# Moving the transposes of x behind the closing scores in a band and stride attention before an MoE, with padded tiles and split loads

## The chip, the cores and the metric

The kernel runs on one core of a Trainium2 chip. A core has five engines with their own instruction queues: TensorE (matmuls and transposes), VectorE, ScalarE, GpSimd and SyncE, which here only issues DMAs. The metric is device time in microseconds. The program was run three times for its median; one further execution was profiled, and all rows of the profile come from that one.

## The reference

Attention with eight batches, eight heads, 576 positions and 64 features; four heads see a local band of 32 positions, four see every 32nd position. The result goes, as 4608 tokens of 512 features, through a router with eight experts of limited capacity (tokens taken in the order of their logits over all tokens) and through two matrices for each expert.

```python
pos = np.arange(S)
rel = pos[:, None] - pos[None, :]
mask_local = (rel >= 0) & (rel < stride)
mask_strided = (rel >= 0) & (pos[None, :] % stride == pos[:, None] % stride)
masks = np.stack([mask_local if h < H // 2 else mask_strided for h in range(H)], axis=0)
scores = scale * np.matmul(q, k.transpose(0, 1, 3, 2))
scores = np.where(masks[None, :, :, :], scores, -1000000000.0)
attn = np.exp(scores - np.max(scores, axis=-1, keepdims=True))
attn = attn / (np.sum(attn, axis=-1, keepdims=True) + 1e-09)
x = np.matmul(attn, v).transpose(0, 2, 1, 3).reshape(B * S, H * D)
...
logits = x @ w_gate
order = np.argsort(-logits.flatten())
...
for e in range(E):
    mask = assigned == e
    out[mask] = np.maximum(x[mask] @ w1[e], 0.0) @ w2[e]
```

## The kernel before

The first third of the time is the attention, the rest routing and experts; the change is in the attention alone, and the engines' order in the rest is the same before and after.

**Units and steps.** Each batch is two units, a strided one (`xs`, `v_s`, `ks`, `qs` in names) and a local one (`xl`, `v_l`, `kl`, `ql`). A unit has two head pairs, and a pair is one step: 32 steps, in the order strided pair 0, strided pair 1, local pair 0, local pair 1, batch after batch. The loop is at lines 612 to 678, and its order is written by hand: no scheduler moves an instruction, each engine runs its queue in that order, and waits only for what an instruction needs. A strided head is cut into tiles of 54 queries (`SQ`), the last of a half being 18 (`SLAST`, from `wide`); a local head into tiles of 32 queries and 64 keys.

**What a step does.** On TensorE, step i: `close_scores` of pair i+1 (`dots`, the scores' last tiles into a two-bank tile `spa`; VectorE then takes the maxima with a transpose, L333), `mix` of pair i for the first head (probabilities `pr` by values, into `po`), `turn` of pair i-1 (x is transposed into `xt`, for the router's logits), `max_t` of pair i+1 (the maxima `mx` are transposed, L339; then VectorE: L342, the cast to bf16 at L344, its error at L345, and `dd` at L347), `mix` for the second head, `open_scores` of pair i+2 (the mask as a matmul, L318, and the first tiles of scores), sometimes a sum of squares `total_v` (L271) or `logits` (L519), and `shift` of pair i+1 (L352: minus the maximum, as a matmul from `dd`). ScalarE then takes the exponential of pair i+1 (L356).

**ScalarE's queue** is, after an exponential: a square of the values (L268, in three steps of four), the copies of the gates (L467 and L455, to `lt`), the finish copy of x to fp16 (L403), and then in the next step the copy of the turn (L438, `keep`). GpSimd subtracts the fp16 copy from x (L404) behind the finish copy, for the low part.

**The banks of the accumulation memory (PSUM).** `ps_a` has two tiles of two banks (`spa`), `po` takes two banks, and `ps_b` has two tiles of one bank (`spb`). The turn uses the tile `a`, which step i opens for the scores of pair i+2; the mask that opens these scores can only be written when ScalarE has copied the turn out of it. The gates (L464), `total_v`, `logits` and the turn of the first pair (`turn_first`) use `spb`. A tile `warm_o` is taken from `ps_b` ahead of the loop (L608) and is written by matmuls without a reader ahead of the first step, between the first ones, and once more in step 31.

**Loads.** SyncE's queue issues the transfers: queries, keys and values of a unit ahead of their use (values to fixed buffers `vbuf`, L299), and ahead of the loop seven tables for the routing (`late_constants`, 0.86 MB with 0.59 MB for `iota`).

Of the kernel before, what the change touches and what calls it, by code (L numbers as in the profile page):

```python
# [8 lines left out]
F32 = mybir.dt.float32  # L9
# [3 lines left out]
AF = mybir.ActivationFunctionType  # L13
# [16 lines left out]
BANK = 512  # L30
OPEN_S, OPEN_L = 1, 3
MAX_FIRST = True
WARM = {(-2, 0): 11, (-1, 0): 3, (-1, 2): 3, (31, 0): 2}
# [99 lines left out]
def band_stride_attention_then_capacity_moe(ctx, tc, qt, kl, ks, nl, ns, wg, w1, w2, cst, out, dbg=None):  # L133
# [83 lines left out]
    with tc.tile_pool(name="ld", bufs=2) as ld, \  # L217
# [13 lines left out]
        po_all = ps_o.tile([128, 2, BANK], F32, name="po")  # L231
        nc.vector.memset(po_all, 0.0)
        for g in "sl":
# [11 lines left out]
        class Unit:  # L245
# [39 lines left out]
            def load(u, parts=(slice(0, 2),), v=True):  # L285
                b, g = u.b, u.g
                if v:
                    u.load_v()
                u.kt = ld.tile([128, 2, u.nk], F32, name="k" + g)
                u.q = ld.tile([128, 2, S], F32, name="q" + g)  # L290
                for p in parts:
                    nc.sync.dma_start(u.kt[:, p], (ks if u.strided else kl)[b, :, p])
                    nc.sync.dma_start(u.q[:, p], qt[b, :, u.p0 + p.start:u.p0 + p.stop])

            def load_v(u):
                u.vn = vbuf[u.g, u.b % 2]
                for f in range(2):
                    r = slice(64 * f, 64 * f + SQ) if u.strided else slice(64 * f + 32, 64 * f + 64)
                    nc.sync.dma_start(u.vn[r], (ns if u.strided else nl)[u.b, f])  # L299

# [20 lines left out]
            def dots(u, p, ts_):  # L321
                for t in ts_:
                    n = u.wide(t)
                    o = u.nq * t
                    for f, h in ((0, 0), (1, 1), (0, 1), (1, 0)):
                        c = HS * f + SQ * t if u.strided else LQ * (2 * t + f)
                        m = n if u.strided else LK
                        r = slice(64 * h, 64 * h + 64)
                        nc.tensor.matmul(u.sp[p][64 * f:64 * f + m, h, o:o + n], u.kt[r, p, c:c + m], u.q[r, p, c:c + n],
                                         start=False, stop=False, skip_group_check=True)  # L330
# [5 lines left out]
            def max_t(u, p):  # L336
                pm = u.sp[p][:, 1, HS:HS + 64]
                for k in range(4):
                    nc.tensor.matmul(pm[32 * k:32 * k + 32], mxb[u.g, p], ident[:, 64 * (k % 2):64 * (k % 2) + 64],  # L339
                                     start=False, stop=False, skip_group_check=True)  # L340
                mr = wk.tile([128, 32], F32, name="mr")
                nc.vector.tensor_reduce(mr, pm.rearrange("r (g c) -> r c g", c=32), axis=AX.X, op=OP.max)  # L342
                mh = wk.tile([128, 32], BF16, name="mh")
                nc.vector.tensor_copy(mh, mr)  # L344
                nc.vector.tensor_tensor(mh[64:], mr[64:], mh[64:], op=OP.subtract)  # L345
                u.dd = wk.tile([128, NB, 32], BF16, name="dd")
                nc.vector.tensor_tensor(u.dd, mh[:, None, :].to_broadcast([128, NB, 32]), bm, op=OP.mult)  # L347

            def shift(u, p):
                df = u.dd.rearrange("r n c -> r (n c)")  # L350
                for h in range(2):
                    nc.tensor.matmul(u.sp[p][:, h, :HS], sel, df[:, HS * h:HS * h + HS], start=False, stop=True,  # L352
                                     skip_group_check=True)
                pr = wk.tile([128, S], F32, name="pr")
                u.pr[p] = pr
                nc.scalar.activation(pr.rearrange("k (h n) -> k h n", h=2), u.sp[p][:, :, :HS], AF.Exp, scale=0.125)  # L356

# [4 lines left out]
            def mix(u, p, h, ts_=None, po=None):  # L362
# [5 lines left out]
                for t in range(u.nt) if ts_ is None else ts_:  # L368
                    n, o = u.wide(t), u.place(t, h)
                    for f in range(2):  # L370
                        j, r = (t, 64 * f) if u.strided else (t // 2, 64 * (t % 2) + 32 * f)
                        k = slice(64 * f, 64 * f + 64)
                        nc.tensor.matmul(po[r:r + n, j - j0], pr[k, o:o + n], u.vn[k, t, 2 * p + h],  # L373
                                         start=(j == j0), stop=(j == j1 - 1), skip_group_check=True)
# [47 lines left out]

            def turn(u, p, po):
                if u.b not in xtb:
                    xtb[u.b] = wk.tile([128, H // 2, S], F32, name="xt")
                for j, c, t, r in u.pieces():
                    x = u.x[r, t, 2 * p:2 * p + 2].rearrange("q h d -> q (h d)")
                    nc.tensor.transpose(po[:, j, c:c + r.stop - r.start], x, ident[r, r])

            def pieces(u):  # L430
                if u.strided:
                    return [(f, SQ * t, t, slice(64 * f, 64 * f + u.wide(t))) for t in range(u.nt) for f in range(2)]
                return [(0, EV + 128 * j, j, slice(0, 128)) for j in range(3)] + \
                    [(1, 128 * (j - 2), j, slice(0, min(128, S - 128 * j))) for j in range(2, u.nx)]

            def keep(u, p, po):
                o = 0 if u.strided else EV
                nc.scalar.activation(xtb[u.b][:, 2 * u.strided + p].rearrange("d (j n) -> d j n", j=2), po[:, :, o:o + HB],  # L438
                                     AF.Copy)

            def turn_first(u, j):
                po = ps_b.tile([128, 512], F32, name="spb")
                for f, c, t, r in u.pieces():
                    if f == j:
                        nc.tensor.transpose(po[:, c:c + r.stop - r.start], u.x[r, t, :2].rearrange("q h d -> q (h d)"),
                                            ident[r, r])
                nc.scalar.activation(xtb[u.b][:, 2, j * HB:(j + 1) * HB], po[:, :HB], AF.Copy)

        HB = S // 2
        EV = HB - 256  # L450
        ltb, xtb = {}, {}
# [125 lines left out]
        for u in todo[2:4]:  # L577
            u.load(v=False)
        late_constants()
        last = 2 * nu - 1  # L580
# [31 lines left out]
        for i in range(-1, 2 * nu):  # L612
            u, n, m = pair(i), pair(i + 1), pair(i + 2)
            if i > 0 and i % 2 == 0 and i // 2 + 3 < nu:
                todo[i // 2 + 3].load()
            if n:
                close_scores(n)
            warm(i, 0)
            for f in drips.get(i, []):
# [10 lines left out]
            if i < last:  # L630
                for f in mids.get(i, []):
                    f(a, b)
                if i > 1:
                    x = pair(i - 1)
                    po = a if m else ps_a.tile([128, 2, 512], F32, name="spa")
                    x[0].turn(x[1], po)
                    x[0].keep(x[1], po)
            if i == last:
# [35 lines left out]
            if i == 2:  # L674
                for j in range(2):
                    todo[0].turn_first(j)
            for f in late.get(i, []) + fills.get(i, []):
# [659 lines left out]
```

## Time and profile before

| what | us |
|---|---|
| median of three runs | 748.49 (742.92 to 751.04) |
| the profiled execution | 744.54 |
| its span | 742.8 |
| first exponential of the loop starts at | 16.3 |
| last exponential of the loop (pair 31) starts at | 230.0 |
| TensorE busy in the span | 634.2 (85%) |
| VectorE busy | 464.5 (63%) |
| ScalarE busy | 348.7 (47%) |

A row of a timeline reads: start, duration (both in us), engine, line, operation, the tile written and the tiles read, shapes, and how many instructions are taken together; in brackets, how long the engine stood idle ahead of it and which instruction ended the wait. A row of waits reads: who waited for whom, us in all, times, and the longest. The matmuls of a group overlap, so that a group's length is best read from its start to the start of the next group.

### The profile page before, as it was taken

Reading aid. Unit: us, or ns where it says so; the run is one execution under the profiler, and the core shown is the slowest. Engines: PE = TensorE matmul, PEld = TensorE weight load, DVE = VectorE, ACT = ScalarE, POOL = GpSimd, SP = SyncE. Lnnn points to the kernel's source line nnn. Section 1 sums busy time; section 2 is a strip of 40 time slices with the busy share of each in tenths; the row PEclk is TensorE's granted clock in tenths of the full one; section 3 lists DMA queues with packets and bytes.
Section 4 is the critical chain, followed back from the end, with each engine's and each line's share of the span. In section 5 each row is a group of like instructions: output and inputs, shape, how many; then the busy total and the mean of one; then the engine's idle time right before and its main releaser. Section 6 shows DMA issues by size and latency. Waiting matters only on the chain.

```text
span 742.8 us, 19700 instructions
## 1 busy us (share of the span) xinstructions
PE 634.2 (85%) x8315; PEld 416.5 (56%) x8315; DVE 464.5 (63%) x1351; ACT 348.7 (47%) x546; POOL 153.8 (21%) x152
## 2 busy tenths in 40 slices
PE   5788886988888449999997998998997997899993
PEld 2565664656666327546645745744843853665741
DVE  3566875867886777967665676666665663653210
ACT  2446466567554045475273284184264354753210
POOL 1042232233143020041050041041023013212011
PEclk9558998999999559999999999999998998899998
DMA  9968585585422063193294085186088069561000
GB/s 212 235 174 233 169 227 146 158 231 143 132 67 66 2 206 107 44 293 83 82 253 84 34 275 112 35 280 105 1 272 147 1 242 222 208 103 51 13 32 32
DMA packets 71836, 102.42 MB, mean 138 GB/s; under 512 B 40604, under 2 KB 48374, under 8 KB 71235
## 3 DMA queue, kind: packets, MB, share of 16 engines
q1 hardware_dynamic: 63667, 79.61, 39.2%
q0 software_dynamic: 7360, 21.15, 10.3%
q8 instruction: 65, 1.06, 0.6%
q10 hardware_dynamic: 720, 0.39, 0.2%
q14 instruction: 24, 0.20, 0.1%
HBM read 73.60 MB, written 18.87 MB: 125 GB/s over the span
## 4 chain that ended last, share of the span: by engine, by line
PE 19%; DMA 16%; issue 13%; DVE 6%; POOL 4%; ACT 2%; SPq 2%; POOLq 0%; ACTq 0%
PE ph L1165 17%; DMA w<-in_w_dram 8%; DMA xg<-x_scr,idx 6%; DMA xt<-xg 3%; POOL xg L1078 2%; POOL out_dram L1224 1%; DVE w2l L1027 1%; ACT jk L1008 1%; SPq L993 1%; DVE hl L1173 1%; SPq L1081 1%; DVE y L1221 0%; ACT yl L1220 0%; DVE cm L830 0%; PE ph L1066 0%
## 5 line engine op out<-in xcount | busy, mean ns | idle before, releaser
L1165 PE MATMUL ph<-xt,w1h 128*128 128x288 f16 (+2 forms) x1024 | 183.2, 296 | 19.7 <-DMA xt<-xg 15.6
L1165 PEld LDWEIGHTS <-w1h 128*128 128x128 f16 x1024 | 99.8, 101 | 52.2 <-issue 13.1
L1224 POOL DMA_INDIRECT out_dram<-y,idx x40 | 43.4, 1085 | 353.6 <-ACT y L1223 323.3
L1165 PE MATMUL ph<-xt,w1l 128*128 128x288 f16 (+2 forms) x512 | 115.3, 295 | 0.0
L1008 ACT ACTIVATE jk<-w 128x1024 f16<-128x1024 f32 x64 | 67.5, 1055 | 77.8 <-DMA w<-in_w_dram 75.6
L1172 ACT ACTIVATE hh<-ph 128x576 f16<-128x576 f32 (+2 forms) x72 | 42.9, 596 | 126.5 <-PE ph L1165 125.1
L1213 PE MATMUL ph<-w2h,hh 128*128 128x512 f16 x256 | 97.0, 379 | 0.0
L1213 PE MATMUL ph<-w2h,hl 128*128 128x512 f16 x256 | 97.0, 379 | 0.0
L1213 PE MATMUL ph<-w2l,hh 128*128 128x512 f16 x256 | 97.0, 379 | 0.0
L1213 PEld LDWEIGHTS <-hh 128*128 128x128 f16 x512 | 48.4, 98 | 60.4 <-issue 10.3
L1173 DVE SCALAR_TENSOR_TENSOR hl<-ph,hh 128x576 f16<-128x576 f32 (+2 forms) x72 | 49.5, 688 | 41.7 <-ACT hh L1172 41.3
L1165 PEld LDWEIGHTS <-w1l 128*128 128x128 f16 x512 | 51.1, 100 | 14.5 <-issue 0.8
L356 ACT ACTIVATE pr<-spa 128x576 f32<-128x576 f32 x32 | 20.8, 651 | 72.6 <-PE spa L352 72.6
L404 POOL TENSOR_TENSOR xos<-xs,xos 118x768 f16<-118x768 f32 x16 | 26.4, 1653 | 128.2 <-ACT xos L403 128.2
L1078 POOL DMA_INDIRECT xg<-x_scr,idx x40 | 42.1, 1052 | 49.4 <-issue 34.4
L1027 DVE SCALAR_TENSOR_TENSOR w2l<-w,w_sw,w2h 128x512 f16<-128x512 f32 x64 | 45.8, 744 | 9.6 <-ACT w2h L1026 9.3
L1027 DVE SCALAR_TENSOR_TENSOR w1l<-w,w_sw,w1h 128x512 f16<-128x512 f32 x64 | 45.9, 748 | 8.4 <-issue 5.1
L1223 ACT ACTIVATE y<-ph,so 128x512 f32<-128x512 f32 x32 | 21.9, 683 | 58.0 <-PE ph L1213 37.3
L1026 ACT ACTIVATE w2h<-w,w_sw 128x512 f16<-128x512 f32 x64 | 41.1, 710 | 6.3 <-DVE w_sw L205 5.6
L1026 ACT ACTIVATE w1h<-w,w_sw 128x512 f16<-128x512 f32 x64 | 41.8, 710 | 3.3 <-DVE ss_e L200 1.8
L373 PE MATMUL po<-v_s,pr 64*54 64x65 f32 (+1 forms) x768 | 35.7, 238 | 6.9 <-ACT pr L356 6.7
L1213 PEld LDWEIGHTS <-hl 128*128 128x128 f16 x256 | 24.9, 97 | 28.5 <-issue 2.7
(614 smaller groups left out, 1020.4 us busy)
## 6 DMA issues: line engine op xcount, KB each, us to landing
w<-in_w_dram SPq DMA_DIRECT2D x64, 512.0 KB
v_s<-in_ns_dram SPq DMA_DIRECT2D x16, 329.1 KB
kl<-in_kl_dram SPq DMA_DIRECT2D x8, 608.0 KB
v_l<-in_nl_dram SPq DMA_DIRECT2D x16, 292.5 KB
ql<-in_qt_dram SPq DMA_DIRECT2D x8, 576.0 KB
x_scr<-xol SPq DMA_DIRECT2D x8, 512.0 KB
ks<-in_ks_dram SPq DMA_DIRECT2D x7, 576.0 KB
qs<-in_qt_dram SPq DMA_DIRECT2D x7, 576.0 KB
```

Source lines behind the costliest of these rows:

```text
L373: nc.tensor.matmul(po[r:r + n, j - j0], pr[k, o:o + n], u.vn[k, t, 2 * p + h], start=(j == j0), stop=(j == j1 - 1), skip_group_check=True)
L404: eng.tensor_tensor(u.xo[:nr, :, 1, c], xf, u.xo[:nr, :, 0, c], op=OP.subtract)
L1008: nc.scalar.activation(jk, wf[:, c * n4:(c + 1) * n4].rearrange("p c f -> p (c f)"), AF.Square, scale=1.41422, accum_out=sq[:, c:c + 1])
L1026: nc.scalar.activation(hi[:, c, f], wf[:, c, f], AF.Copy, scale=s_)
L1027: nc.vector.scalar_tensor_tensor(lo[:, c, f], wf[:, c, f], s_, hi[:, c, f], op0=OP.mult, op1=OP.subtract)
L1078: nc.gpsimd.indirect_dma_start(out=xg[:n], out_offset=None, in_=x_rows, in_offset=bass.IndirectOffsetOnAxis(ap=idx[:n, t:t + 1], axis=0))
L1165: nc.tensor.matmul(tile_[:, j, :w], wt[:, d, f * 128:(f + 1) * 128], xt[:, d // 2, xx, d % 2, c], start=(k == 0), stop=(k == 3 * DC - 1))
L1172: nc.scalar.activation(hv, src, AF.Relu)
L1173: nc.vector.scalar_tensor_tensor(lv, src, 0.0, hv, op0=OP.max, op1=OP.subtract)
L1213: nc.tensor.matmul(py, a[:, f, ts_], w[:, f], start=(k == 0), stop=(k == len(todo) - 1))
L1223: nc.scalar.activation(y, py, AF.Copy, scale=so[:, t:t + 1])
L1224: st = nc.gpsimd.indirect_dma_start(out=out_rows, out_offset=bass.IndirectOffsetOnAxis(ap=idx[:n, t:t + 1], axis=0), in_=y[:n], in_offset= ...
```

## The change

The edits, in the order of the diff:

- The strided keys are in two fixed buffers `ktb` and the probabilities in two fixed buffers `prb`, each 36 columns longer, with zeros and ones behind the end (four memsets on GpSimd); `po` starts as ones and not as zeros. With this the last strided tile is 54 wide like the others: in the dots the keys' side (54 rows written, 18 columns), in the mix the queries, in the turn the columns.
- The strided values come as 48 and 6 rows for each half and not as 54: four DMAs for two.
- The cast of the maxima to bf16 is a maximum of the tile with itself, with two operands.
- `turn` stands behind `close_scores` and ahead of the first `mix`. It makes two pieces, each in a tile of `ps_b`, with a copy each by ScalarE: 288 columns each in a strided unit, 384 and 192 in a local one, which takes five transposes for six. `pieces`, `keep` and `turn_first` are gone; in step 2 both pairs of the first unit are turned.
- `late_constants` is called in step 13 and not ahead of the loop.

```diff
@@ constants and start @@
+CONST_AT = 13
...
-        nc.vector.memset(po_all, 0.0)
+        nc.vector.memset(po_all, 1.0)
+        ktb = [ld.tile([128, 2 * S + SQ - SLAST], F32, name=f"ks{i}", bufs=1) for i in range(2)]
+        prb = [wk.tile([128, S + SQ - SLAST], F32, name=f"pr{i}", bufs=1) for i in range(2)]
+        for i in range(2):
+            nc.gpsimd.memset(ktb[i][:, 2 * S:], 0.0)
+            nc.gpsimd.memset(prb[i][:, S:], 1.0)
@@ load_v @@
                 for f in range(2):
-                    r = slice(64 * f, 64 * f + SQ) if u.strided else slice(64 * f + 32, 64 * f + 64)
-                    nc.sync.dma_start(u.vn[r], (ns if u.strided else nl)[u.b, f])
+                    for i, n in ((0, 48), (48, SQ - 48)) if u.strided else ((0, 32),):
+                        r = 64 * f + (i if u.strided else 32)
+                        nc.sync.dma_start(u.vn[r:r + n], (ns if u.strided else nl)[u.b, f, i:i + n])
@@ dots @@
-                        m = n if u.strided else LK
+                        m = SQ if u.strided else LK
@@ max_t @@
-                nc.vector.tensor_copy(mh, mr)
+                nc.vector.tensor_tensor(mh, mr, mr, op=OP.max)
@@ shift @@
-                pr = wk.tile([128, S], F32, name="pr")
-                u.pr[p] = pr
+                pr = u.pr[p] = prb[p]
@@ mix @@
-                        nc.tensor.matmul(po[r:r + n, j - j0], pr[k, o:o + n], u.vn[k, t, 2 * p + h],
+                        nc.tensor.matmul(po[r:r + u.nq, j - j0], pr[k, o:o + u.nq], u.vn[k, t, 2 * p + h],
@@ turn @@
-            def turn(u, p, po):
+            def turn(u, p):
                 if u.b not in xtb:
                     xtb[u.b] = wk.tile([128, H // 2, S], F32, name="xt")
-                for j, c, t, r in u.pieces():
-                    x = u.x[r, t, 2 * p:2 * p + 2].rearrange("q h d -> q (h d)")
-                    nc.tensor.transpose(po[:, j, c:c + r.stop - r.start], x, ident[r, r])
+                x = u.x[:, :, 2 * p:2 * p + 2].rearrange("q t h d -> q t (h d)")
+                cut = HB if u.strided else 384
+                for j in range(2):
+                    po = ps_b.tile([128, 512], F32, name="spb")
+                    if u.strided:
+                        for t in range(u.nt):
+                            r = slice(64 * j, 64 * j + SQ)
+                            nc.tensor.transpose(po[:, SQ * t:SQ * t + SQ], x[r, t], ident[r, r])
+                    else:
+                        for t in range(3 * j, 3 + 2 * j):
+                            nc.tensor.transpose(po[:, 128 * t - cut * j:128 * t - cut * j + 128], x[:, t], ident)
+                    c = slice(cut * j, S if j else cut)
+                    nc.scalar.activation(xtb[u.b][:, 2 * u.strided + p, c], po[:, :c.stop - c.start], AF.Copy)
@@ the loop @@
+            if i == CONST_AT:
+                late_constants()
             if n:
                 close_scores(n)
+            if 2 < i < last:
+                x = pair(i - 1)
+                x[0].turn(x[1])
...
-                if i > 1:
-                    x = pair(i - 1)
-                    po = a if m else ps_a.tile([128, 2, 512], F32, name="spa")
-                    x[0].turn(x[1], po)
-                    x[0].keep(x[1], po)
...
             if i == 2:
-                for j in range(2):
-                    todo[0].turn_first(j)
+                for p in range(2):
+                    todo[0].turn(p)
```

What this does to TensorE's queue in a step whose turn is local, with the gates of the step before ahead of it. A row is the line, the operation, written and read tiles, what is written (partitions by columns), how often, and the semaphores an instruction waits for (`Activation` is ScalarE, `DVE` VectorE). Before:

```order
L464 MATMUL spb<-xt,wgp 32x288 x3
L329 MATMUL spa<-qs,ks 54x54 x16
L329 MATMUL spa<-qs,ks 18x18 x4
L373 MATMUL po<-v_l_141,pr 32x65 [waits DVE_49,Activation_49]
L373 MATMUL po<-v_l_141,pr 32x65 x17
L428 MATMUL spa<-ident,xl 128x128 [waits PE_49]
L428 MATMUL spa<-ident,xl 128x128 x4
L428 MATMUL spa<-ident,xl 128x64
L339 MATMUL spa<-ident,mx_s_127 32x64 [waits DVE_49]
L339 MATMUL spa<-ident,mx_s_127 32x64 x3
L373 MATMUL po<-v_l_141,pr 32x65 x18
L318 LDWEIGHTS ident_b
```

After:

```order
L461 MATMUL spb<-xt,wgp 32x288 x3
L337 MATMUL spa<-qs,ks_127 54x54 x16
L337 MATMUL spa<-qs,ks_127 54x18 x4
L443 MATMUL spb<-ident,xl 128x128 [waits DVE_49,PE_49,Activation_49]
L443 MATMUL spb<-ident,xl 128x128 x2
L443 MATMUL spb<-ident,xl 128x128 [waits Activation_49]
L443 MATMUL spb<-ident,xl 128x128
L380 MATMUL po<-v_l_149,pr_130 32x65 x18
L347 MATMUL spa<-ident,mx_s_135 32x64 [waits DVE_49]
L347 MATMUL spa<-ident,mx_s_135 32x64 x3
L380 MATMUL po<-v_l_149,pr_130 32x65 x18
L326 LDWEIGHTS ident_b
```

The turn has moved from behind the first mix to ahead of it, from `spa` to `spb`, and each of its two pieces waits for ScalarE.

ScalarE's queue between two exponentials, in a step whose turn is strided. Before:

```order
L356 ACTIVATE pr<-spa 128x576
L268 ACTIVATE jk,vsq_115<-v_l_141 32x2304
L467 ACTIVATE lt<-spb,ss_s 64x288
L455 ACTIVATE lt<-spb,ss_s 64x18x16
L403 ACTIVATE xos<-xs 118x6x128
L438 ACTIVATE xt<-spa 128x576
```

After:

```order
L363 ACTIVATE pr_129<-spa 128x576
L274 ACTIVATE jk,vsq_115<-v_s_141 128x1536
L410 ACTIVATE xos<-xs 118x6x128
L445 ACTIVATE xt<-spb 128x288 x2
L363 ACTIVATE pr_130<-spa 128x576
L274 ACTIVATE jk,vsq_115<-v_l_149 32x2304
L464 ACTIVATE lt<-spb,ss_s 64x288
L452 ACTIVATE lt<-spb,ss_s 64x18x16
L410 ACTIVATE xos<-xs 118x6x128
L445 ACTIVATE xt<-spb 128x288 x2
```

Two copies of half the columns stand where one stood, in the same place behind square, gates and finish copy.

SyncE's queue at the start, before:

```order
L299 DMA v_s_129<-in_ns_dram 54x1560 x2
L299 DMA v_l_137<-in_nl_dram 32x2340 x2
L572 DMA wg_sb<-in_wg_dram 128x32
L573 DMA sum_g<-in_c_sum_g_dram 128x8
L292 DMA kl<-in_kl_dram 128x1216
```

After:

```order
L307 DMA v_s_137<-in_ns_dram 48x1560
L307 DMA v_s_137<-in_ns_dram 6x1560
L307 DMA v_s_137<-in_ns_dram 48x1560
L307 DMA v_s_137<-in_ns_dram 6x1560
L307 DMA v_l_145<-in_nl_dram 32x2340 x2
L569 DMA wg_sb<-in_wg_dram 128x32
L570 DMA sum_g<-in_c_sum_g_dram 128x8
L298 DMA kl<-in_kl_dram 128x1216
```

Two more issues stand ahead of what follows the values of a strided unit.

More of the change, by code (lines that the diff above doesn't have):

```diff
@@ L288, in load @@
                     u.load_v()
-                u.kt = ld.tile([128, 2, u.nk], F32, name="k" + g)
+                u.kt = ktb[b % 2] if u.strided else ld.tile([128, 2 * u.nk], F32, name="kl")
                 u.q = ld.tile([128, 2, S], F32, name="q" + g)
                 for p in parts:
-                    nc.sync.dma_start(u.kt[:, p], (ks if u.strided else kl)[b, :, p])
+                    nc.sync.dma_start(u.kt[:, p.start * u.nk:p.stop * u.nk].rearrange("q (p n) -> q p n", n=u.nk),
+                                      (ks if u.strided else kl)[b, :, p])
                     nc.sync.dma_start(u.q[:, p], qt[b, :, u.p0 + p.start:u.p0 + p.stop])
@@ L326, in dots @@
                         c = HS * f + SQ * t if u.strided else LQ * (2 * t + f)
-                        m = n if u.strided else LK
+                        m = SQ if u.strided else LK
                         r = slice(64 * h, 64 * h + 64)
-                        nc.tensor.matmul(u.sp[p][64 * f:64 * f + m, h, o:o + n], u.kt[r, p, c:c + m], u.q[r, p, c:c + n],
+                        nc.tensor.matmul(u.sp[p][64 * f:64 * f + m, h, o:o + n], u.kt[r, p * u.nk + c:p * u.nk + c + m], u.q[r, p, c:c + n],
                                          start=False, stop=False, skip_group_check=True)
@@ L353, in shift @@
                                      skip_group_check=True)
-                pr = wk.tile([128, S], F32, name="pr")
-                u.pr[p] = pr
-                nc.scalar.activation(pr.rearrange("k (h n) -> k h n", h=2), u.sp[p][:, :, :HS], AF.Exp, scale=0.125)
+                pr = u.pr[p] = prb[p]
+                nc.scalar.activation(pr[:, :S].rearrange("k (h n) -> k h n", h=2), u.sp[p][:, :, :HS], AF.Exp, scale=0.125)
             def slots(u, ts_):
@@ L368, in mix @@
                 for t in range(u.nt) if ts_ is None else ts_:
-                    n, o = u.wide(t), u.place(t, h)
+                    o = u.place(t, h)
                     for f in range(2):
@@ L421, in store @@
                     nc.sync.dma_start(xs[n:, 0], xo[:S - n, n // 128])
-            def turn(u, p, po):
+            def turn(u, p):
                 if u.b not in xtb:
                     xtb[u.b] = wk.tile([128, H // 2, S], F32, name="xt")
-                for j, c, t, r in u.pieces():
-                    x = u.x[r, t, 2 * p:2 * p + 2].rearrange("q h d -> q (h d)")
[L428 to L447, printed above, removed]
+                x = u.x[:, :, 2 * p:2 * p + 2].rearrange("q t h d -> q t (h d)")
@@ L449, in band_stride_attention_then_capacity_moe @@
         HB = S // 2
-        EV = HB - 256
         ltb, xtb = {}, {}
@@ L578, in band_stride_attention_then_capacity_moe @@
             u.load(v=False)
-        late_constants()
         last = 2 * nu - 1
```

## The prediction

> **What bounds it now.** I read the page first, whose costliest groups show where each engine's idle time lies, then the waits in the loop (30 to 230 us), then ScalarE's and TensorE's timelines over one cycle of four steps.
>
> ```profile
> ACT pr L356 <- PE spa L352: 65.2, 29, 4.1
> ...
> PE spa L318 <- ACT xt L438: 15.7, 12, 1.9
> ...
> PE spa L352 <- DVE dd L347: 11.0, 13, 1.4
> ```
> ScalarE waits for TensorE, not the other way: TensorE's order sets the pace, and it loses 15.7 us to masks that wait for the copy of the turn and 11.0 us to shifts that wait for `dd`. The change aims at both. The second stage is issued as before and starts from the last batch's logits, so I let what the loop gains or loses reach the end one to one.
>
> ScalarE over a cycle (start, duration). From exponential to exponential is one step:
>
> ```profile
> 40.85 0.65 ACT L356 ACTIVATE pr<-spa 128x576 f32<-128x576 f32 x1 [2.51 <-PE spa L352]
> ...
> 154.36 0.65 ACT L356 ACTIVATE pr<-spa 128x576 f32<-128x576 f32 x1 [1.70 <-PE spa L352]
> ...
> 161.03 0.65 ACT L356 ACTIVATE pr<-spa 128x576 f32<-128x576 f32 x1 [1.32 <-PE spa L352]
> ...
> 167.28 0.65 ACT L356 ACTIVATE pr<-spa 128x576 f32<-128x576 f32 x1 [2.96 <-PE spa L352]
> 167.83 1.48 ACT L268 ACTIVATE jk<-v_s 128x1536 f16<-128x1536 f32 x1
> 169.29 0.83 ACT L403 ACTIVATE xos<-xs 118x768 f16<-118x768 f32 x1
> 170.03 0.64 ACT L438 ACTIVATE xt<-spa 128x576 f32<-128x576 f32 x1
> 173.14 0.65 ACT L356 ACTIVATE pr<-spa 128x576 f32<-128x576 f32 x1 [2.48 <-PE spa L352]
> 173.82 2.12 ACT L268 ACTIVATE jk<-v_l 32x2304 f16<-32x2304 f32 x1
> 176.57 0.50 ACT L455 ACTIVATE lt<-spb,ss_s 64x288 f32<-64x288 f32 x1
> 177.96 0.65 ACT L438 ACTIVATE xt<-spa 128x576 f32<-128x576 f32 x1
> 179.70 0.65 ACT L356 ACTIVATE pr<-spa 128x576 f32<-128x576 f32 x1 [1.09 <-PE spa L352]
> 184.41 0.65 ACT L438 ACTIVATE xt<-spa 128x576 f32<-128x576 f32 x1
> 187.11 0.65 ACT L356 ACTIVATE pr<-spa 128x576 f32<-128x576 f32 x1 [2.05 <-PE spa L352]
> ...
> 230.04 0.65 ACT L356 ACTIVATE pr<-spa 128x576 f32<-128x576 f32 x1 [2.13 <-PE spa L352]
> ```
> Steps are 6.25 (161.03 to 167.28), 5.86, 6.56 and 7.41 us: a cycle of 26.08. The 28 steps from 40.85 to 230.04 take 189.2 us, seven cycles of 27.0. In the second and third step a square of 2.1 us and the gates' two copies stand ahead of the finish copy and the turn's copy.
>
> TensorE in the same cycle:
>
> ```profile
> 172.65 0.41 PE L352 MATMUL spa<-dd,sel 128*128 128x288 bf16 x2 [1.04 <-DVE dd L347]
> ...
> 174.44 0.76 PE L373 MATMUL po<-v_l,pr 64*32 64x65 f32 x36
> 175.13 0.68 PE L428 MATMUL spa<-ident,xs 54*128 54x54 f32 x12
> 175.74 0.32 PE L339 MATMUL spa<-ident,mx_l 128*32 128x64 f32 x8
> ...
> 187.97 1.00 PE L373 MATMUL po<-v_s,pr 64*54 64x65 f32 x24 [0.18 <-ACT pr L356]
> 188.89 0.97 PE L428 MATMUL spa<-ident,xl 128*128 128x128 f32 x6
> 189.79 0.32 PE L339 MATMUL spa<-ident,mx_s 128*32 128x64 f32 x8
> ...
> 191.80 1.27 PE L519 MATMUL spb<-sum_g,lt 128*128 128x8 f32 x10
> ```
> From start to start: one mix 0.69 (local) or 0.92 (strided), a strided turn 0.61, a local one 0.90, and 2.01 from the maxima's transposes over second mix (strided), masks and opening dots to what follows them. The exponential follows 0.49 after the shift's start (172.65 to 173.14).
>
> **The turn: one bank, not two.** `warm_o` is one of the two tiles of `ps_b`, and is still written at step 31, so the other bank carries every other `spb` tile: turn pieces, gates, totals, logits. In the order after, each second piece waits for ScalarE, which is its first piece's copy, and the first piece behind a gates step waits for the copies of the gates. The trace has this wait once, at the first unit's turn:
>
> ```profile
> 40.74 1.00 PE L445 MATMUL spb<-ident,xs 54*128 54x54 f32 x6
> 42.24 0.99 PE L445 MATMUL spb<-ident,xs 54*128 54x54 f32 x6 [0.50 <-ACT xt L447]
> ```
> ```profile
> 41.77 0.41 ACT L447 ACTIVATE xt<-spb 128x288 f32<-128x288 f32 x1 [0.28 <-PE spb L445]
> ```
> 0.5 us there, with ScalarE free. In the loop ScalarE isn't free, and the pieces now stand ahead of the mix, so what they wait delays mix, maxima, masks and shift. I lay out each step of the cycle, T its exponential's start, with the durations above, a copy at 0.41 (288 columns; 0.49 for 384, between that and the 0.65 of 576), and `dd` ready 1.54 us after the maxima's transposes start, from the one above and this:
>
> ```profile
> 176.82 0.46 DVE L347 TENSOR_TENSOR dd<-mh,bm 128x576 bf16<-128x576 bf16 x1
> ```
> - Step from 167.28: piece 0 ends at T+1.05; its copy stands behind square and finish, T+2.75 to 3.16; piece 1 to 3.53, mix to 4.45, maxima to opening dots 2.01, 6.46, exponential 0.49 later: 6.95 for 5.86, +1.09.
> - Step from 173.14: dots end at T+1.30 (where the mix of 174.44 starts now), but the bank is held until the gates' second copy ends, T+3.93. Piece 0 to 4.24; copy behind the finish copy, 4.82 to 5.23; piece 1 to 5.60; mix 6.29; `dd` 7.83; exponential 8.34 for 6.56: +1.78.
> - Step from 179.70: the same wait to T+4.0, local pieces (0.45, 0.30): copy 4.71 to 5.20, piece 1 to 5.56, mix 6.25, `dd` 7.79, the rest of TensorE's work to 8.0; exponential 8.51 for 7.41: +1.10.
> - Step from 187.11: gates don't stand ahead; piece 0 ends at T+1.30, its copy, behind exponential and finish copy (0.83 at most, as at 169.29), at T+2.05, piece 1 at 2.41, mix at 3.34, where mix and turn ended at T+2.68 (189.79) before; the rest of the step is as it was: +0.66.
>
> Together 4.63 for the cycle. The masks' and the shift's waits that go are in it: both fall away in each step. Seven cycles are 32.4; steps 29 and 30 have no square and step 3 no gates, so that I take off 1.1, 1.2 and 1.0: **+29**. Seven cycles of 26.08 are 182.6, not 189.2: 6.6 us are waits of other cycles (transfers in the early ones), which a slower loop may hide. Bounds 0 and -6.6; as they lie mostly early, where much else is late, I take **-2**. Step 2 now has four pieces in the chain shown at 40.74 (1.5 us each) for two: +3, bounds +1 and +5.
>
> **The clock.** TensorE idles 2.1 us in the first of these steps, and 3.6 and 3.4 us with only a piece between in the next two. Three adjoining windows (PE busy, ..., PEclk the third number from the end):
>
> ```profile
> 173.03:176.44 3.41, 3.41 (x145) 2.63 (x146) 2.58 (x5) 3.25 (x4) 0.00 (x0) 1.00 0.99 215
> 176.44:179.85 3.41, 1.50 (x36) 0.80 (x28) 1.96 (x6) 2.25 (x5) 1.64 (x1) 1.00 0.86 246
> 179.85:183.26 3.41, 3.41 (x87) 2.46 (x80) 1.36 (x3) 3.35 (x5) 1.87 (x3) 0.50 0.68 189
> ```
> Behind a window with 1.9 us idle the clock is halved for a window. The step in it took 7.41; the same step a turn of the loop earlier, 154.36 to 161.03, 6.67: 0.74 us for a cold window. Two more such gaps a cycle, 14 in all: **+10.4**; none or twice that are the bounds. The Trainium skill ("TensorE: Matmul & The Clock Gate", "Why this matters for your kernels") says only idle gaps of over some 3 us bring the clock down; no single gap here would reach that, and by it this term is 0. The trace above disagrees, with 1.9 us.
>
> **The other parts.** Maxima: the cast becomes a maximum of two SBUF operands. Its neighbour on the same data is such an instruction:
>
> ```profile
> 170.26 1.62 DVE L344 CAST mh<-mr 128x32 bf16<-128x32 f32 x1
> ```
> ```profile
> 170.20 1.65 POOL L404 TENSOR_TENSOR xos<-xs,xos 118x768 f16<-118x768 f32 x1 [6.41 <-ACT xos L403]
> ```
> ```profile
> L345 DVE TENSOR_TENSOR mh<-mr,mh x32: 189/189/1580, 9.2 to 228.8; 64x32 bf16<-64x32 f32 x32
> ```
> The cast took 1.62 beside GpSimd's subtraction, and the two-operand form of L345, 0.19 as a rule, was stretched as far once or more, to 1.58. So the edit saves nothing by itself: 0, bounds -11.0 (the whole wait for `dd`) and +1. The Trainium skill ("SBUF — State Buffer", "Who interferes with whom") says that a VectorE instruction with two SBUF inputs contends with a GpSimd instruction that reads SBUF; it speaks against the edit, and L345 agrees. In my layout the collision mostly goes anyway, since the maxima come later than the subtraction.
>
> Wider last tiles, by the mixes of 54 and of 18 columns:
>
> ```profile
> L373 PE MATMUL po<-v_s,pr 64*54 64x65 f32 x560 | 22.8, 227 | 0.9 <-ACT pr L356 0.7
> ...
> L373 PE MATMUL po<-v_s,pr 64*18 64x65 f32 x112 | 8.3, 226 | 0.0
> ```
> The narrow ones are no cheaper: 74 ns of busy time each for 41. Part of that is the tail of their group, in which they stand last, for the whole group of 24 takes 0.92, 38 each. So 0, bounds -3.7 (112 times the 33 ns) and +1; the memsets lie in the wait for the first data. Values and start:
>
> ```profile
> 14.83 1.48 ACT L268 ACTIVATE jk<-v_s 128x1536 f16<-128x1536 f32 x1 [10.09 <-DMA v_s<-in_ns_dram]
> ```
> ```profile
> 22.94 0.87 PE L329 MATMUL spa<-ql,kl 64*64 64x32 f32 x24 [1.67 <-DMA ql<-in_qt_dram]
> ```
> The first values could land up to some 5 us sooner, but the local queries, landing at 22.9, are then what is waited for, and 24 more issues stand in SP's queue, two of them ahead of these queries: -1, bounds -5 and +1. The constants move to step 13; their first reader stands at step 24: 0, bounds -1 and +2.
>
> Sum: 29 - 2 + 3 + 10.4 - 1 = +39.4, from 744.54 (the span and 1.7 us around it): **784 us**. The median of the runs, 748.49, lies 0.5% over that one execution, so 784 is 4.7% over the median.
>
> **Rivals.**
> 1. Clock untouched (idle time in pieces too short to matter): 744.5 + 29 = 773.5. For: windows with small gaps stay at 1.00; against: the row at 179.85. Chance 0.18.
> 2. Clock worse: four cold windows a cycle more instead of two, since two steps out of three now begin behind a gap: +20.8 for +10.4, 794.3. Chance 0.15.
> 3. Faster: the pieces get two banks after all, or ScalarE's copies come promptly, so that no piece waits. Then the 15.7 us at the masks go, about half of the 11.0 at the shifts and 1 at the start: 744.5 - 22 = 722. It decides where the pieces' waits in a cycle (10 us in my layout: 2.1 + 3.6 + 3.4 + 0.8) come below (15.7 + 5.5) / 7 = 3.0. Against: the order names the waits, and the chain of 40.74 shows one. Chance 0.04.
> 4. Nothing gained or lost: the edit does not do what it says ("two other banks" is one), but ScalarE's copies come soon enough that the pieces' waits are just the 3.0 us a cycle that go elsewhere: 744.5 + 3 (step 2) - 1 = 746.5. For: in the step from 187.11 the wait is 0.8; against: the square and the gates' copies ahead in two steps of four. Chance 0.03.
>
> **How the numbers follow.** The forecast has 0.60, the rivals 0.18, 0.15, 0.04 and 0.03. The range reaches down past rival 1 by the -6.6 and the start's -5 (764), and up past rival 2 by the +2 of step 2 and what the copies' order may add (806); it leaves out some 0.15. A measurement of this kernel tells 1% from no change: slower 0.93, same 0.03, faster 0.04.
>
> **What would show it.** Right: waits of TensorE's turn (L440, L443) for the copy L445 and the gates' copy L452 of some tens of us in all; the masks' wait (L326) near zero; steps of about 7, 8.3, 8.5 and 7 us, and cold ones above; lower PEclk in slices 3 to 13; a last exponential near 270. Wrong: masks or shift as before with no wait at the turn (rival 3); clock as before with those waits (rival 1); a second stage whose length changes.

## The result and the profile after

| | before | after |
|---|---|---|
| median, us | 746.94 (742.92 to 751.04, 4 runs) | 805.32 (800.54 to 817.75, 4 runs) |
| the profiled execution / its span | 744.54 / 742.8 | 807.9 / 806.1 |

The ratio is 1.076, with a 95% interval of 1.066 to 1.086: slower by 58 us, where 39 were forecast. The median lies just inside the forecast's range of 764 to 806, the profiled execution just over it. In the profiled executions the first exponential starts at 13.48 (16.32 before), the fourth at 39.02 (40.85), the last at 298.68 (230.04). So the 28 steps between them take 259.7 us for 189.2, 70.5 more; the start gives 1.8 us, and the second stage is 5.4 us shorter (507.4 for 512.8), which makes the 63.3 between the two spans.

The granted clock of TensorE in 40 slices of the span (a digit is tenths), before (the 28 steps are slices 3 to 13) and, with the span, after (slices 3 to 15):

```profile
PEclk9558998999999559999999999999998998899998
```
```profile
span 806.1 us, 19705 instructions
PEclk9658867667867596599999999899899999899998
```

What TensorE waited for in the loop after (20 to 300 us; us in all, times, longest). L440 and L443 are the turn's transposes, L445 its copy, L452 the gates' second copy, L360 the shift:

```profile
PE spb L440 <- ACT xt L445: 17.4, 17, 1.9
PE spb L443 <- ACT lt L452: 16.4, 6, 2.8
PE spb L440 <- ACT lt L452: 14.9, 7, 2.6
PE spb L443 <- ACT xt L445: 11.4, 14, 3.4
PE spa L326 <- issue: 4.6, 1, 4.6
...
PE spa L360 <- DVE dd L355: 1.7, 3, 0.9
```

The masks (L326) no longer wait for the copy of the turn (their one wait, 4.6 us, ended at 37.6, ahead of the 28 steps, and the profile shows no releaser for it), and the wait for `dd` fell from 11.0 to 1.7, as the change meant. In their place stand 60.1 us at the turn, at the two releasers that the order had named. Two steps on TensorE, those from 209.38 and 218.87:

```profile
210.06 0.57 PE L440 MATMUL spb<-ident,xs 54*128 54x54 f32 x6
212.58 0.89 PE L440 MATMUL spb<-ident,xs 54*128 54x54 f32 x6 [1.95 <-ACT xt L445]
213.39 1.55 PE L380 MATMUL po<-v_s,pr 64*54 64x65 f32 x24
...
218.12 0.66 PE L360 MATMUL spa<-dd,sel 128*128 128x288 bf16 x2
...
219.55 0.90 PE L337 MATMUL spa<-ql,kl 64*64 64x32 f32 x48
222.84 0.89 PE L440 MATMUL spb<-ident,xs 54*128 54x54 f32 x6 [2.38 <-ACT lt L452]
224.22 0.89 PE L440 MATMUL spb<-ident,xs 54*128 54x54 f32 x6 [0.50 <-ACT xt L445]
225.04 1.30 PE L380 MATMUL po<-v_l,pr 64*32 64x65 f32 x36
```

and on ScalarE:

```profile
209.38 0.65 ACT L363 ACTIVATE pr<-spa 128x576 f32<-128x576 f32 x1 [3.99 <-PE spa L360]
209.93 1.48 ACT L274 ACTIVATE jk<-v_s 128x1536 f16<-128x1536 f32 x1
...
212.13 0.40 ACT L445 ACTIVATE xt<-spb 128x288 f32<-128x288 f32 x1
...
218.87 0.65 ACT L363 ACTIVATE pr<-spa 128x576 f32<-128x576 f32 x1 [4.96 <-PE spa L360]
...
222.29 0.50 ACT L452 ACTIVATE lt<-spb,ss_s 64x288 f32<-64x288 f32 x1
...
229.53 0.65 ACT L363 ACTIVATE pr<-spa 128x576 f32<-128x576 f32 x1 [3.98 <-PE spa L360]
```

The second piece of the first of these steps starts at T+3.20 (3.22 in the prediction's layout), the first piece of the next at T+3.97 (3.93). Up to there the layout holds to 0.1 us. Behind the gap it doesn't: the mix that took 0.92 from start to start takes 1.48, and the step ends at 9.49 and not at 6.95. The reason is in adjoining windows over the same steps (PE busy first, PEclk third from the end):

```profile
209.04:212.45 3.41, 1.59 (x56) 1.24 (x54) 2.58 (x6) 3.07 (x5) 0.15 (x1) 0.99 0.29 100
212.45:215.86 3.41, 3.28 (x50) 2.88 (x52) 0.42 (x2) 0.49 (x2) 1.50 (x1) 0.50 0.00 0
215.86:219.27 3.41, 3.41 (x54) 1.92 (x50) 2.06 (x5) 0.40 (x1) 0.00 (x0) 0.51 0.48 109
219.27:222.69 3.42, 1.19 (x56) 0.79 (x48) 1.34 (x2) 3.36 (x5) 0.00 (x0) 0.99 0.96 186
222.69:226.10 3.41, 2.76 (x48) 2.48 (x48) 0.00 (x0) 1.76 (x4) 2.07 (x2) 0.50 0.61 251
226.10:229.51 3.41, 3.41 (x68) 1.88 (x64) 2.33 (x7) 0.00 (x0) 1.43 (x3) 0.51 0.69 173
```

Each of these two gaps is followed by two windows at half the clock ("cold" windows), not one. The window right behind the gap isn't wholly busy (3.28 of 3.41, and 2.76), and the clock stays down; the next one is, and the clock comes back. In this execution the clock drops 17 times between 60 us and the end of the loop: eleven times for two windows, four times for one, twice for four. How busy a cold window is doesn't settle by itself whether the clock comes back. Later in the same execution a cold window that was busy throughout was followed by another:

```profile
249.94:253.35 3.41, 3.41 (x52) 3.00 (x54) 0.57 (x3) 0.41 (x1) 1.34 (x1) 0.50 0.00 0
253.35:256.76 3.41, 3.41 (x52) 1.77 (x48) 2.12 (x6) 0.56 (x1) 0.00 (x0) 0.50 0.00 0
```

and in the kernel before one with 3.23 us busy was not:

```profile
70.62:74.03 3.41, 3.23 (x63) 1.57 (x59) 0.00 (x0) 2.67 (x2) 2.29 (x4) 0.50 0.72 227
74.03:77.45 3.42, 3.24 (x105) 2.45 (x99) 3.09 (x5) 2.57 (x6) 1.35 (x1) 1.00 0.27 79
```

The cycle from 209.38 to 246.71 is 9.49, 10.66, 10.68 and 6.50 us, 37.3 for the 26.1 of before.

### The profile page after: what moved, and what is told of

The parts are those of the page before. It is cut to its first block, busy times and chain, and to the rows that moved or that the text cites. A ratio compares the mean times of both kernels' runs of the same rounds, so it can differ in the third digit from the quotient of the medians.

```text
span 806.1 us, 19705 instructions
## 1 busy us (share of the span) xinstructions
PE 668.4 (83%) x8298; PEld 441.5 (55%) x8301; DVE 451.3 (56%) x1351; ACT 351.9 (44%) x575; POOL 151.7 (19%) x156
## 4 chain that ended last, share of the span: by engine, by line
PE 17%; issue 16%; DMA 11%; DVE 5%; POOL 3%; SPq 2%; ACT 1%; POOLq 0%; DVEq 0%; ACTq 0%
PE ph L1161 13%; DMA xg<-x_scr,idx 5%; DMA w<-in_w_dram 4%; PE ph L1209 2%; DMA xt<-xg 2%; SPq L1077 2%; POOL out_dram L1220 2%; POOL xg L1074 1%; DVE w2l L1023 1%; DMA out_dram<-y,idx 1%; SPq L989 1%; DVE hl L1169 1%; PE ph L1203 1%; DVE w1l L1023 1%; ACT jk L1004 0%
## 5 line engine op out<-in xcount | busy, mean ns | idle before, releaser
L350 DVE TENSOR_REDUCE mr<-spa 128x32 f32<-128x64 f32 x32 | 7.1, 222 | 84.3 <-PE spa L347 84.2
L440 PE MATMUL spb<-ident,xs 54*128 54x54 f32 x192 | 23.6, 275 | 32.3 <-ACT xt L445 17.4
```

The lines of the kernel that those rows point to most:

```text
L440: nc.tensor.transpose(po[:, SQ * t:SQ * t + SQ], x[r, t], ident[r, r])
```

## The experiments

All ratios below are to the kernel before on the same chip, with 95% intervals.

**The turn back in its old place.** The changed kernel, less one part:

```diff
-            if 2 < i < last:
-                x = pair(i - 1)
-                x[0].turn(x[1])
...
+                if i > 1:
+                    x = pair(i - 1)
+                    po = a if m else ps_a.tile([128, 2, 512], F32, name="spa")
+                    x[0].turn(x[1], po)
+                    x[0].keep(x[1], po)
```

> The changed kernel with the turn back in its old place and bank; wider tiles, two-operand maxima, split values and later constants stay. Theory (the turn's place with its one bank costs all of the loss, the other edits gain about 3 us at the start): 738 to 746, cycle of four steps 25 to 26.5. Rival (wider tiles or the two-operand maxima cost a part of the loss): over 755.

741.21 us, ratio 0.992 (0.987 to 0.996). All of the loss is the turn's; the other edits together gain about 0.8%.

**The turn's new place alone.** The same part put into the kernel before, and nothing else of the change.

```diff
+            if 2 < i < last:
+                x = pair(i - 1)
+                x[0].turn(x[1])
...
-                    x[0].turn(x[1], po)
-                    x[0].keep(x[1], po)
```

> The kernel before with the turn's new place, pieces and single bank alone; narrow tiles, cast, whole values and early constants stay. Theory (the place makes all of the loss and the other parts gain under 1%): steps of about 6.5, 9.5, 10.7 and 10.7, 805 to 818. Rival (the place is bad only together with the wider tiles or the two-operand maxima): under 795.

814.26 us, ratio 1.090 (1.081 to 1.098). The place with its single bank does it by itself: 66 us over the 748.39 of before. With the other parts it was 58.

**Only the idle time filled.** Matmuls of zeros into the bank of `warm_o`, which nothing reads, where TensorE waits; each piece still waits as before.

```diff
+FILL = {("s", 0): (0, 8, 0), ("s", 1): (10, 3, 0), ("l", 0): (10, 3, 0), ("l", 1): (0, 3, 0)}
...
+                for _ in range(FILL[u.g, p][0] if 1 <= u.b < B - 1 else 0):
+                    nc.tensor.matmul(warm_o, warm_i[:, :128], warm_i, start=True, stop=True, skip_group_check=True)
```

> The changed kernel with matmuls of zeros into the warming tile where TensorE waits at the turn (10 ahead of the first piece behind a gates step and 3 or 8 ahead of the second, batches 1 to 6): waits and order stay, only the idle time is filled. Theory (about 42 us of the loss are the halved clock behind the gaps): steps of 6.5, 7, 8.4 and 8.6, a cycle of 30.5 for 37.3, the clock near 1.00: 762 to 775. Rival (the longer matmuls have another cause, or the fillers only lengthen the queue): 800 or over.

772.43 us, ratio 1.031 (1.020 to 1.042), inside the theory's numbers. The exponentials of one cycle in this run:

```profile
216.91 0.65 ACT L364 ACTIVATE pr<-spa 128x576 f32<-128x576 f32 x1 [3.99 <-DVE xs L399]
223.84 0.65 ACT L364 ACTIVATE pr<-spa 128x576 f32<-128x576 f32 x1 [2.71 <-PE spa L361]
232.35 0.65 ACT L364 ACTIVATE pr<-spa 128x576 f32<-128x576 f32 x1 [2.22 <-PE spa L361]
240.88 0.65 ACT L364 ACTIVATE pr<-spa 128x576 f32<-128x576 f32 x1 [2.47 <-PE spa L361]
247.50 0.65 ACT L364 ACTIVATE pr<-spa 128x576 f32<-128x576 f32 x1 [3.99 <-PE spa L361]
```

Steps of 6.93, 8.51, 8.53 and 6.62 us; the layout had 6.95, 8.34, 8.51 and 6.91. Three windows over the loops, of before, of after and of this run (clock third from the end):

```profile
60.00:235.00 175.00, 145.69 (x3892) 104.88 (x3887) 131.48 (x318) 102.79 (x145) 54.49 (x50) 0.94 0.55 156
```
```profile
60.00:299.00 239.00, 183.41 (x3912) 132.18 (x3908) 119.94 (x316) 104.81 (x167) 52.20 (x46) 0.75 0.42 118
```
```profile
60.00:260.00 200.00, 191.73 (x4137) 123.72 (x4138) 118.98 (x319) 104.92 (x167) 52.22 (x46) 0.99 0.50 142
```

More work on TensorE made the loop 39 us shorter, since it kept the clock. A mean of 0.75 over 239 us is half the clock for 119.5 us, 35 windows of 3.41; 0.94 over 175 us is 6, 0.99 over 200 about 1. So some 34 windows cost 39 us, an estimate of 1.15 each. Work and waits without the clock make the rest: the 28 steps take 220.6 us here (39.43 to 259.99), 31.4 more than before, where the prediction's 29 - 2 + 3 make 30.

**Filled between the pieces only,** in the two steps behind gates; the gap ahead of the first piece stays.

```diff
+FILL = {("s", 0): (0, 0, 0), ("s", 1): (0, 2, 0), ("l", 0): (0, 2, 0), ("l", 1): (0, 0, 0)}
```

> The changed kernel with two filling matmuls between the two pieces of the turn in the steps behind gates only, batches 1 to 6; the gap of 2.4 us ahead of the first piece stays. Theory (a halved clock lasts until a whole window of 3.41 us is busy, and the wait of 0.5 us between the pieces makes it last a second window): one cold window for two in these two steps, which fall from 10.7 to about 9.7, the other two steps as they are: 790 to 799. Rival (the clock stays down for two windows behind a gap of this length, whatever follows): 803 or over.

803.12 us, ratio 1.071 (1.062 to 1.080): the rival's number. The steps were 10.96 and 10.59, the mean clock in the loop 0.74. But the run doesn't decide, because the window behind the gap was still not filled: it began at 224.52, 0.1 us ahead of the first piece, and the records show 2.97 of its 3.41 us busy.

```profile
224.62 0.88 PE L443 MATMUL spb<-ident,xs 54*128 54x54 f32 x6 [2.33 <-ACT lt L457]
225.84 0.63 PE L448 MATMUL spb<-warm_i 128*128 128x512 bf16 x1 [0.34 <-issue]
226.40 0.88 PE L443 MATMUL spb<-ident,xs 54*128 54x54 f32 x6
```

So closing the 0.5 us between the pieces did not take the second cold window away. Whether what was still idle in the window kept the clock down, or something else, this run can't tell. (One of the two fillers has no record here, so the 0.34 may be the other.)

**Two banks.** The tile `warm_o` is only used ahead of the loop's first steps, and the two matmuls of step 31 take a tile of their own; so `ps_b` has both its banks for the rest.

```diff
+            t = warm_o if i < 1 else ps_b.tile([128, 512], F32, name="spb")
             for _ in range(WARM.get((i, k), 0)):
-                nc.tensor.matmul(warm_o, warm_i[:, :128], warm_i, start=True, stop=True, skip_group_check=True)
+                nc.tensor.matmul(t, warm_i[:, :128], warm_i, start=True, stop=True, skip_group_check=True)
```

> The changed kernel, but the tile of the warming matmuls is given back after the loop's first steps (that of step 31 gets a tile of its own), so that the turn's pieces have two banks in turn. Theory (the single bank makes the waits): no piece waits for the copy of the other; only the second piece behind a gates step still waits for the gates' copies, about 2.3 us, with one cold window behind it; steps of about 5.6, 4.8, 7.5 and 7.7, in all 735 to 755. Rival (the place ahead of the mix costs, whatever the banks): over 785.

758.28 us, ratio 1.016 (1.008 to 1.024): a little over the theory's range, far from the rival. What TensorE waits for between 60 and 240 us:

```profile
PE spb L440 <- ACT lt L452: 12.6, 6, 2.1
PE spb L443 <- ACT lt L452: 12.6, 6, 2.3
PE spa L360 <- DVE dd L355: 5.9, 6, 1.2
```

The waits for the turn's own copy are gone, those for the gates' copies stay. The typical steps are 5.6 to 6.0, 5.7 to 5.9 (7.35 twice), 8.55, and 7.42 or about 8.7. The step of 8.55 has a mean clock of 0.80, which is 3.4 us at half: one cold window, wholly busy, for the two of the changed kernel. Behind the second gap of a cycle there is none in half the cycles.

**The squares behind the copies, one bank.** The squares stand ahead of everything that the pieces wait for on ScalarE; here they are issued in the next step, behind the turn.

```diff
-                        at(2 * j - V_AT + f, lambda u=u, f=f: u.square_v(f), True)
+                        square(2 * j - V_AT + f, lambda u=u, f=f: u.square_v(f), True)
...
+        def square(step, f, early):
+            drips.setdefault(step + 1, []).append(f) if step > 1 else at(step, f, early)
```

> The changed kernel with its single bank, and only the squares issued behind the turn's copies. Theory (what the pieces wait for on ScalarE is mostly the square ahead of their copies; the bank alone costs about a us a step): steps of about 6.5, 5.8, 6.0 and 6.4, few cold windows: 725 to 750. Rival (the single bank by itself makes most of the loss, whatever ScalarE has ahead): 775 or over.

751.64 us, ratio 1.013 (1.004 to 1.022), just above the range. Its four runs spread from 742.50 to 756.58, and those of before from 737.59 to 759.00, so that a loss of this size is not well settled. The undisturbed steps are 6.64, 5.70, 6.25 and 6.79, a cycle of 25.4. Waits for the copy of the other piece remain, 9.0 and 7.6 us between 60 and 230, none over 0.8. So the bank is not the whole cause: either remedy alone, this one (805 to 752) or the second bank (805 to 758), takes most of the loss away, and neither takes all of the waits.

**Both,** the second bank and the late squares. "The run before" in the expectation is the one with two banks.

> As the run before, and the squares of the values are issued behind the turn's copies instead of ahead of the gates' copies, so that these copies come 2.1 us (1.5 in one step) sooner. Theory: no wait of over 0.5 us at the turn is left, the clock stays at 1.00 in the loop, a cycle of 22 to 24 us for 26.1 before: 715 to 730. Rival (ScalarE or VectorE becomes the bound when TensorE doesn't wait): 735 to 745.

729.71 us, ratio 0.979 (0.970 to 0.989): 2.1% faster than before, and 9% faster than the changed kernel. Its four runs, 722.09 to 735.27, all lie under those of before on that chip, 742.06 to 764.45. Waits between 60 and 215 us:

```profile
PE spa L360 <- DVE dd L355: 9.1, 11, 1.1
PE spa L337 <- issue: 5.8, 4, 2.4
PE spb L277 <- ACT jk L274: 3.9, 4, 1.1
```

No wait at the turn for a copy is among them. A cycle without a cold window is 23.2 (6.15, 5.77, 5.70 and 5.57 from 119.28 on); the mean clock between 60 and 215 us is 0.96, not the theory's 1.00. The last exponential starts at 215.4. Neither part alone measured under the kernel before; together they do. Whether the late squares would also speed up the kernel before, with the turn in its old place, was not run, so that the gain over before isn't shown to come from the new place.

**What bounds the faster version.** Two tries at its remaining waits. First the sum of squares behind the shift:

```diff
-            if i in mids2:
+            if i == 1 and i in mids2:
                 mids2[i].total_v(b)
...
                 n[0].shift(n[1])
+            if i in mids2 and i > 1:
+                mids2[i].total_v(b)
```

> The version with two banks and the squares behind the copies, and the sum of the squares behind the shift instead of ahead of it. Theory: TensorE's wait for the square (4.6 us) goes off the path to the exponential: 2 to 6 us less than that version, 724 to 728. Rival (the shift then waits for VectorE or ScalarE as long): no difference.

735.94 us, ratio 0.987 (0.979 to 0.996): no gain. The wait for the square is gone from the list of the longest, that for `dd` is 13.4 us in the loop where it was 12.5. Then VectorE's copies of the local values behind the normalisation:

```diff
-                        drips.setdefault(2 * j + COPY_AT[k], []).append(lambda u=u, k=k: u.copy_v(k))
+                        copies.setdefault(2 * j + COPY_AT[k], []).append(lambda u=u, k=k: u.copy_v(k))
...
+            for f in copies.get(i, []):
+                f()
             if n:
                 n[0].shift(n[1])
```

> The version with two banks and the squares behind the turn's copies, and VectorE's copies of the local values issued behind the normalisation of a step instead of ahead of its maxima. Theory (what TensorE still waits for is dd, 12 us in that version, behind these copies on VectorE): the wait for dd falls under 6 us, 5 to 8 us less than that version, 720 to 726. Rival (VectorE's queue is late by as much at the next maxima, or the mix waits for the copies): no difference or more.

735.05 us, ratio 0.986 (0.980 to 0.992). The wait for `dd` did fall, to 2.9 us, but the time didn't. Some steps got shorter (4.58 for 5.70), others longer: two of 8.85 and 9.55 with cold windows in them (mean clock 0.61 and 0.63). The miss isn't settled; the intervals of the three versions overlap.

**The other parts alone,** each put into the kernel before. The two-operand maximum:

```diff
-                nc.vector.tensor_copy(mh, mr)
+                nc.vector.tensor_tensor(mh, mr, mr, op=OP.max)
```

> The kernel before with the two-operand maximum alone. Theory (both forms contend with GpSimd's subtraction): longest about 1.6 us as before, the wait of the shifts for dd 10 to 12 us, no difference within 0.4%. Rival (the cast alone was what GpSimd stretched): no instance over 0.3 us, the wait for dd near 0, up to 11 us less.

743.95 us, ratio 1.000 (0.995 to 1.004). The edit moves nothing, and its row says why (least, median and longest ns):

```profile
L344 DVE TENSOR_TENSOR mh<-mr x32: 191/193/1629, 9.0 to 228.0; 128x32 bf16<-128x32 f32 x32
```

It is stretched as far as the cast was, 1.62. (In the kernel before 11 of the 32 casts were stretched, each beside GpSimd's subtraction.) In the changed kernel the same instruction was never stretched:

```profile
L352 DVE TENSOR_TENSOR mh<-mr x32: 191/192/194, 9.7 to 297.2; 128x32 bf16<-128x32 f32 x32
```

That is the order's doing: the maxima come behind GpSimd's subtraction there. In the run with the turn's place alone, which has the cast, the longest is 0.30. The collision isn't wholly gone, though: `dd` (L355), never over 0.46 before, took 2.77 us once in the changed kernel, beside the subtraction.

Split values and later constants:

```diff
-                    r = slice(64 * f, 64 * f + SQ) if u.strided else slice(64 * f + 32, 64 * f + 64)
-                    nc.sync.dma_start(u.vn[r], (ns if u.strided else nl)[u.b, f])
+                    for i, n in ((0, 48), (48, SQ - 48)) if u.strided else ((0, 32),):
+                        r = 64 * f + (i if u.strided else 32)
+                        nc.sync.dma_start(u.vn[r:r + n], (ns if u.strided else nl)[u.b, f, i:i + n])
...
-        late_constants()
...
+            if i == 13:
+                late_constants()
```

> The kernel before with two parts of the change alone: values as 48 and 6 rows, constants at step 13. Theory (the first values land sooner and the rest of the start follows): first exponential near 13.3 instead of 16.3, the loop as before: 3 us less, 743 to 746 where before is 747. Rival (the gain is lost again by the local queries and the later loads): no difference within 0.2%.

744.99 us, ratio 1.001 (0.997 to 1.005). The first exponential starts at 13.93 for 16.32, the fourth at 41.05 for 40.85, and the last at 230.09 for 230.04: the 2.4 us are lost again within three steps, as the rival had it.

The wider tiles:

```diff
-                        m = n if u.strided else LK
+                        m = SQ if u.strided else LK
...
-                        nc.tensor.matmul(po[r:r + n, j - j0], pr[k, o:o + n], u.vn[k, t, 2 * p + h],
+                        nc.tensor.matmul(po[r:r + u.nq, j - j0], pr[k, o:o + u.nq], u.vn[k, t, 2 * p + h],
```

> The kernel before with the wider last tiles alone (54 for 18 in dots, mix and turn, with the padded buffers). Theory (a narrow instruction costs TensorE about as much as a wide one): strided steps 0 to 0.2 us shorter, 0 to 4 us less in all. Rival (the wider tiles make the whole 0.8% by which the change without its turn is faster): 5 to 8 us less.

743.54 us, ratio 0.993 (0.990 to 0.997), 4.9 us less. In the profile one step of four is 0.2 us shorter (6.03 to 6.18 for 6.25 to 6.40), 1.5 us in all. Where the rest of the gain lies isn't shown: in the profiled execution, 746.99 us, the 28 steps take 192.4 us, 3.3 more than before.

## Why the prediction was right in direction, and what was mis-sized

- **The number: inside the range, with luck.** 805.32 lies 0.7 us under the upper end, 806. That end stood some 10 us over the rival with the worse clock for "what the copies' order may add", which was not worked out; what filled it was the clock. And the loop alone lost 70.5 us, its last exponential at 298.68 where near 270 was expected; a shorter second stage (5.4) and start (1.8) brought the two profiled executions to 63.3 apart.
- **One bank, waits at the turn for ScalarE: right.** The releasers are those named, 60.1 us in all, and the masks' wait for the copy and nearly all of the shift's are gone. Undoing it (two banks) takes the waits for the own copy away.
- **The layout of the four steps, +29: right.** With the clock kept up, the steps came out within 0.3 us of it, and the 28 steps 31.4 us longer, for 30 with the step of four pieces and what was to be hidden. Of these two, the step of four pieces was under-sized: 16.84 for 10.54 before, 6.3 more, beyond the bound of 5, since its first local turn waited 3.4 us for its copy.
- **The clock, +10.4: the step that failed, by size.** It measured 39 us. "Two more such gaps a cycle, 14 in all" was wrong in the count: the first step's gap of 2 us counts too, and most gaps bring two cold windows. Between 60 us and the loop's end there are some 35, where the kernel before has 6 and the run with the idle time filled, whose steps are the layout's, has 1. "0.74 us for a cold window" was wrong in the price, by the estimate of 1.15: it was taken from a step in which a wait gave way. The step that it was compared with, 154.36 to 161.03, had a mean clock of 0.88 itself; but one of the same kind at 1.00, 205.93 to 212.61, takes 6.68 us, so that the price there stays. What made it small is the masks' wait, first in the step at 1.00, then in the cold one:

```profile
211.34 0.41 PE L318 MATMUL spa<-mask_s,ident_b 128*128 128x288 bf16 x2 [1.71 <-ACT xt L438]
```
```profile
185.11 0.41 PE L318 MATMUL spa<-mask_s,ident_b 128*128 128x288 bf16 x2 [0.23 <-ACT xt L438]
```

  In the new order hardly anything waits behind the turn, so that nearly all of a longer matmul is on the path. The rival with a worse clock had the mechanism right and stopped at four windows a cycle; the cycle from 209.38 has six.
- **The page's rule of the Trainium skill on idle gaps** ("TensorE: Matmul & The Clock Gate", "Why this matters for your kernels", that gaps of over some 3 us bring the clock down) doesn't agree with these traces: gaps of 1.95 and 2.38 us did.
- **Maxima, 0: right**, and the collision at the maxima went by the order, as laid out.
- **Wider tiles, 0 within -3.7 and +1:** they gained 4.9 us, beyond the bound, though the interval (2.1 to 7.8) reaches inside it.
- **Start, -1:** near enough; the first exponential came 2.8 us sooner, the fourth 1.8. But the run with the turn's place alone, without these parts, has the fourth at 38.59, 2.3 sooner, and the time of the two parts alone is unchanged. The "24 more issues" are 16: the DMAs of the strided values go from 16 to 32.
- **The second stage one to one:** not quite. It was 5.4 us shorter after the change. Among the profiled executions of these kernels it was 504 to 515 us, with no pattern by edit, so that this is put down to no part of the change.

## What to carry to other kernels

Count the buffers that really rotate: a tile that is used once more at the end of a loop holds its bank all the way, and a pool of two is then a pool of one. Where a producer is moved ahead of the work that used to cover its consumer, look at what stands ahead of that consumer in its engine's queue; here moving the square of 1.5 to 2.3 us from ahead of the copies was worth as much as the second bank. And price a gap on TensorE with the matmuls behind it: a cold stretch measured where a wait gave way is too cheap for a place where none is left.

## What the hardware showed beyond that

The granted clock changed on a raster of 3.41 us, and in the loops it was 0.50 or 1.00 for a whole window of it. Counted over all 14 profiled executions, from 35 us to the end of the loop: at full clock, all 80 windows in which TensorE was busy for less than 1.79 of 3.41 us were followed by a cold one, and 40 of the 537 busier ones; at half clock, none of the 93 windows with under 3.19 us busy brought the clock back, 13 of 25 between that and 3.39 did, and 121 of the 137 that were busy throughout. So a busy window is what the clock nearly always came back behind, but what decides the rest isn't shown. Idle time up to 0.8 us at a time, some 17 us of it in the run with one bank and late squares, left most steps at 1.00 (mean clock 0.92). Filling the waits with useless matmuls took 33 us off the median (805.32 to 772.43).
